# Windowed attention and a gated convolution in one kernel: its hand-written orders and the engines of its small copies are exchanged

## The chip, the cores and the metric

The kernel runs on one core of a Trainium2 chip. A core has five engines that run their own instruction streams and wait for each other by semaphores: TensorE (PE in the profile: matmuls and transposes by matmul, PEld its weight loads), VectorE (DVE), ScalarE (ACT), GpSimd (POOL) and SyncE (SP), which here issues every DMA. The metric is the device time of one execution in microseconds (us). The kernel before takes 554.26 us, the median of three runs (554.05, 554.26, 555.79).

## The reference

```
scores = (q @ k^T) / sqrt(64)                       # 8 batches, 8 heads, 576 tokens, 64 wide, fp32
scores = where(0 <= rel < 128, scores - slope[h] * |rel|, -1e9)   # rel = query - key position
attn   = exp(scores - max) / (sum + 1e-9)
x      = (attn @ v), heads joined                    # (8, 576, 512)
h      = max(x @ w_in, 0)                            # 512 -> 1024
conv   = sum_k conv_w[k] * h shifted by k - 1        # three taps along the tokens, zeros at a batch's ends
out    = (h * sigmoid(conv)) @ w_out                 # 1024 -> 512
```

## The kernel before

The 8 x 576 tokens are 36 tiles of 128 tokens for the attention and 18 chunks of 256 tokens for the second part. A chunk is worked in four steps, each on two blocks of 128 of the 1024 columns, so there are 72 steps; the text writes a step's number behind its piece.

**The attention of a tile.** q and k come by DMA (from tile 8 on in groups of nine blocks of 32 tokens, `rp_late`, 32 DMAs to a group, two buffers). DVE turns them over (`STREAM_TRANSPOSE`, L365, piece TQ), PE makes the scores of a tile in four PSUM tiles `sc` (L413, piece S), DVE masks each (L457 and L463, piece MP) and adds the bias with the maximum's work (L473, two instructions to a tile, piece MB), ACT takes the exponentials (L481, two instructions to a piece X), and a product with the reciprocal sums, on POOL from L501, normalizes (piece N). The weights are then turned over by a way through memory: DVE transposes them (L534, TE), a DMA writes them twice, 1 MB, into `scr` (L544, WE), eight DMAs to a pair of tiles read them back along a diagonal (L558, SE), POOL cuts them to the window (L568 and L572, CE), and PE multiplies with v (L591, AV). The first eight tiles take a shorter way with transposes on PE.

**The second part of a step.** PE makes the up-product `p` (L697, 12 matmuls to a block, 24 to a step, piece UH; L692 for the first four steps), as a sum of a high and two low parts of fp32, and ACT the relu `hh` (L709, HH). ACT takes the middle tap (L717, Z), DVE the two outer taps (L732, CA and CB, four instructions to a step), ACT the tanh that gives the sigmoid (L739, TH), DVE the gate (L747, GT), ACT the high part `gh` (L186, GH), POOL the low part `gl` (L768, GL), and PE the down-product `o` (L804, D). After four steps the chunk's result is copied to `ob` and stored (L830, OB). `zp`, which holds the taps, is one buffer: the next step's middle tap waits for the gate of this one. Scores, up-products and the attention's products all take turns in one pool of five PSUM tiles, so that a matmul into the next tile also waits for whoever reads the tile that is five turns older.

**What sets the order.** Nothing is scheduled by a planner: every engine runs its instructions as the program emits them. Three strings of pieces say what is emitted in which order, and one helper runs them:

```
emit(OPENING)
for t in range(FIRST, NT, 2):                 # FIRST = 8, NT = 36: 14 times, two tiles and four steps each
    emit(PERIOD, t, 2 * (t - FIRST) + 10, "P:")
emit(TAIL, NT, 2 * (NT - FIRST) + 10, "T:")
```

A number behind a name counts from t or from the step: in the period for t = 20, TQ4 is tile 24, WE3 tile 23 and UH4.1 the second block of step 38. The opening holds the first eight tiles, the splitting of the weights into high and low parts (pieces CL, RS, LW, V, H, W, from the weight DMAs F) and the first steps; LG4 issues the next four DMAs of a group. For a small copy or a cast that more than one engine can do, `pick(usual, other)` takes the second engine where the piece's name stands in the set `OTHER`.

Of the kernel before, what the change touches and what calls it, by code (L numbers as in the profile page):

```python
# [16 lines left out]
P = 128  # L17
# [5 lines left out]
def tile_alibi_window_attention_conv_glu(  # L23
# [265 lines left out]
    TURN = FIRST  # L289
# [86 lines left out]
    def window(t):  # L376
        return (t * P) % S, 1, 0
# [45 lines left out]
    def place(t, u, a):  # L423
# [11 lines left out]
        if t >= TURN:  # L435
            place_window(t, ps)
            return
# [30 lines left out]
    def add_bias(t, u, a):  # L468
        e, st, pss = sms[t, u]
        of = pss[a][:, :, BK:WIN] if t >= TURN else pss[a][:, :, window(t)[1], :]  # L470
# [383 lines left out]
    def emit(pieces, t=0, s=0, part=""):  # L854
# [16 lines left out]
        GH6 GH7 GH8 GL5 H14 H15 H16 H2 H5 H9 HH0.0 HH3.1 HH4 HH5 KC7 LW0 LW1 LW10 LW14 LW4 LW8 N2.0 N3.1 N8.0  # L871
        QV2.0 QV3.0 RL1.0 RL3.1 RL5.1 RL6.1 T:GH-1 T:GH0 T:GH1 T:GH2 T:GH3 T:GH4 T:GH5.0 T:GH5.1 T:GL-1 T:GL0
        T:GL4 T:GL5.0 T:HH0 T:HH2 T:HH4 T:HH5.1 T:XL-1 W11 W13 W14 W9 XH0 XH2 XH6
# [47 lines left out]
    AV-1 HH0 Z0.0 UH1.1 XA-1 UH1.0 XS-1 D-2 Z0.1 CA0.1 CA0.0 CB0.1 CB0.0 TH0 GT0 XH-1 XL-1 GH-1 XF-1 GL-1 HH1 Z1.1  # L921
    Z1.0 CA1.1 CA1.0 GH0 CB1.0 GL0 CB1.1 UH3.0 TH1 GT1 UH2.0 UH2.1 HH2 Z2.0 Z2.1 CA2.1 CA2.0 CB2.1 CB2.0 TH2 GT2 GH2
# [39 lines left out]
```

## Time and profile before

| | |
|---|---|
| median of three runs | 554.26 us |
| the profiled execution's own time | 554.5 us |
| its span, from the first instruction to the last | 552.8 us |
| PE busy | 546.0 us, 99% of the span |
| DVE, ACT, POOL busy | 446.8, 384.4, 342.5 us |
| share of the chain of waits on PE | 91% |
| granted clock of PE, mean | 0.999 |

The 1.7 us between the span and the execution's own time lie before the first and behind the last instruction. PE stands still for 6.8 us of the span, the time ahead of its first matmul and that of the last store among them.

### The profile page before, as it was taken

How to read it: one execution, taken by the hardware profiler on the slowest of the kernel's cores; microseconds unless marked ns; L12 is line 12 of the kernel's file. 1: busy time of each engine (PE TensorE's matmuls, PEld its weight loads, DVE VectorE, ACT ScalarE, POOL GpSimd, SP SyncE). 2: the span in 40 equal slices, each digit the busy share in tenths (PEclk: the TensorE clock that was granted, in tenths of full speed). 3: DMA queues.
4: the chain of work that ended last, by engine and by line, in shares of the span. 5: the costliest groups of instructions: out<-in, count | busy, mean ns of one | idle time of the engine just before them, and what ended most of it. 6: DMA issues, size and time to landing. Idle time of an engine off the chain costs nothing.

```text
span 552.8 us, 17956 instructions
## 1 busy us (share of the span) xinstructions
PE 546.0 (99%) x6689; PEld 479.2 (87%) x6689; DVE 446.8 (81%) x1505; ACT 384.4 (70%) x1149; POOL 342.5 (62%) x450
## 2 busy tenths in 40 slices
PE   9999999999999999999999999999999999999997
PEld 8788886988888888888888888898989898989986
DVE  8899999888789977887596987788879987665763
ACT  5899876775867676868586776767676777664441
POOL 1787977594656575666558493948473948483241
PEclk9999999999999999999999999999999999999999
DMA  9987764546776767767676768676768664540102
GB/s 209 229 242 204 202 104 81 164 156 169 157 205 142 231 156 205 184 205 169 183 201 175 196 178 207 163 219 184 190 176 205 179 162 148 159 155 1 39 0 78
DMA packets 206779, 91.39 MB, mean 165 GB/s; under 512 B 178380, under 2 KB 192996, under 8 KB 206692
## 3 DMA queue, kind: packets, MB, share of 16 engines
q1 hardware_dynamic: 206692, 90.24, 62.5%
q8 instruction: 53, 0.87, 0.7%
q14 instruction: 34, 0.28, 0.2%
HBM read 51.40 MB, written 38.80 MB: 163 GB/s over the span
## 4 chain that ended last, share of the span: by engine, by line
PE 91%; DMA 2%; DVE 2%; SPq 2%; issue 1%; ACT 0%; DVEq 0%
PE o L804 34%; PE p L697 33%; PE av L591 7%; PE sc L413 6%; PE p L692 3%; PE o L794 3%; PE av L631 3%; PE sc L398 2%; SPq L341 1%; DMA wst<-in_moe_w_in_dram 1%; PE pa L507 1%; PE pt L351 1%; DVE zp L732 1%; DMA rp_late<-in_q_dram 1%; SPq L315 0%
## 5 line engine op out<-in xcount | busy, mean ns | idle before, releaser
L697 PE MATMUL p<-ring,wi 128*128 128x256 f32 x1088 | 195.8, 282 | 0.7 <-ACT hh L709 0.7
L732 DVE SCALAR_TENSOR_TENSOR zp<-hh,cw,zp 128x256 f32<-128x256 f32 (+7 forms) x384 | 160.4, 418 | 29.2 <-ACT zp L717 19.6
L697 PEld LDWEIGHTS p<-ring,wi 128*128 128x128 f32 x1088 | 168.4, 188 | 4.9 <-ACT hh L709 1.1
L697 PE MATMUL p<-ring,wl 128*128 128x256 f32 x544 | 152.3, 280 | 0.0
L768 POOL TENSOR_TENSOR gl<-z,gh 128x512 fp32r<-128x512 f32 x63 | 81.5, 1294 | 100.9 <-ACT gh L186 68.4
L481 ACT ACTIVATE e<-e,st 128x128 f32<-128x128 f32 x288 | 111.8, 391 | 4.2 <-DVE st L473 3.1
L804 PE MATMUL o<-wo,gh 128*128 128x512 f32 x270 | 110.0, 407 | 0.0
L501 POOL TENSOR_TENSOR e<-e,st 128x512 f32<-128x512 f32 x69 | 72.2, 1056 | 58.9 <-DVE st L493 54.1
L804 PE MATMUL o<-wo,gl 128*128 128x512 f32 x270 | 105.7, 392 | 0.0
L804 PE MATMUL o<-wl,gh 128*128 128x512 f32 x270 | 105.2, 390 | 0.0
L697 PEld LDWEIGHTS p<-ring,wl 128*128 128x128 f32 x544 | 102.7, 189 | 0.0
L739 ACT ACTIVATE zp<-zp 128x512 f32<-128x512 f32 (+1 forms) x73 | 42.2, 578 | 62.9 <-DVE zp L732 61.5
L717 ACT ACTIVATE zp<-hh,cw 128x256 f32<-128x256 f32 x144 | 68.5, 476 | 20.0 <-DVE z L747 10.0
L473 DVE CUSTOM_DVE_ANT_0 e<-sc,bias 128x128 f32<-128x128 f32 x288 | 66.8, 284 | 1.7 <-PE pa L507 0.2
L747 DVE SCALAR_TENSOR_TENSOR z<-zp,hh 128x512 f32<-128x512 f32 (+1 forms) x73 | 49.0, 671 | 21.1 <-ACT zp L739 20.2
L804 PEld LDWEIGHTS o<-wo,gh 128*128 128x128 f32 x270 | 50.6, 188 | 16.6 <-issue 6.7
L804 PEld LDWEIGHTS o<-wo,gl 128*128 128x128 f32 x270 | 50.5, 187 | 11.5
L804 PEld LDWEIGHTS o<-wl,gh 128*128 128x128 f32 x270 | 50.8, 188 | 9.3
L709 ACT ACTIVATE hh<-p 128x512 f32<-128x512 f32 (+2 forms) x69 | 39.5, 572 | 25.2 <-PE p L697 20.3
L481 ACT ACTIVATION_READ_ACCUMULATOR e<-e,st 128x1 f32 x288 | 54.5, 189 | 0.0
L186 ACT CAST gh<-z 128x512 fp32r<-128x512 f32 x58 | 35.6, 614 | 15.3 <-DVE z L747 15.3
L572 POOL TENSOR_SCALAR_AFFINE_SELECT rr<-rr 128x512 f32<-128x512 f32 x56 | 40.2, 722 | 3.4
(131 smaller groups left out, 882.5 us busy)
## 6 DMA issues: line engine op xcount, KB each, us to landing
scr<-eb SPq DMA_DIRECT2D x28, 1024.0 KB, 5.1
rr<-scr SPq DMA_DIRECT2D x112, 128.0 KB, 3.7
out_dram<-ob SPq DMA_DIRECT2D x17, 512.0 KB, 3.4
rv<-in_v_dram SPq DMA_DIRECT2D x32, 256.0 KB, 3.4
rp_late<-in_k_dram SPq DMA_DIRECT2D x192, 36.0 KB, 2.9
rp_late<-in_q_dram SPq DMA_DIRECT2D x192, 36.0 KB, 2.2
wst<-in_moe_w_in_dram SPq DMA_DIRECT2D x8, 512.0 KB, 7.0
wst<-in_moe_w_out_dram SPq DMA_DIRECT2D x8, 512.0 KB, 4.8
```

The lines of the kernel that those rows point to most:

```text
L473: nc.vector.tensor_tensor_reduce(out=e[:, j, :], in0=of[:, g, :], in1=bias[:, u * HU + j, :], scale=-0.125, scalar=FAR, op0=ALU.add, op1=A ...
L481: nc.scalar.activation(out=e[:, j, :], in_=e[:, j, :], func=AF.Exp, bias=st[:, 0, j : j + 1], scale=-1.0, accum_out=st[:, 1, j : j + 1],)
L501: eng.tensor_tensor(out=e, in0=e, in1=st[:, 2, :].unsqueeze(2).to_broadcast([P, HU, P]), op=ALU.mult)
L572: nc.gpsimd.affine_select(out=r, in_=r, pattern=[[BK, 2], [0, H], [1, BK]], compare_op=ALU.is_ge, fill=0.0, base=q0, channel_multiplier=-1,)
L697: nc.tensor.matmul(ps, a[:, part], ring[:, i, cc, cols], start=cc == 0 and n == 0, stop=cc == NCC - 1 and n == 2)
L709: nc.scalar.activation(out=to, in_=ps, func=AF.Relu, scale=0.5)
L717: nc.scalar.activation(out=zps[s][:, ff, :], in_=hhs[s][:, ff, 1 : 1 + CW], func=AF.Copy, scale=cw[:, 1, f : f + 1])
L732: nc.vector.scalar_tensor_tensor(out=z[:, ff, a:cut], in0=hh[:, ff, a + kk : cut + kk], scalar=cw[:, kk, f : f + 1], in1=z[:, ff, a:cut], ...
L739: nc.scalar.activation(out=zps[s][:, ff], in_=zps[s][:, ff], func=AF.Tanh)
L747: nc.vector.scalar_tensor_tensor(out=zgs[s][:, ff], in0=zps[s][:, ff], scalar=1.0, in1=hhs[s][:, ff, 1 : 1 + CW], op0=ALU.add, op1=ALU.mult,)
L768: eng.tensor_tensor(out=gl, in0=zgs.pop(s), in1=as32(gh), op=ALU.subtract)
L804: nc.tensor.matmul(to, a[:, ff, ms], w[:, part], start=first and n == 0, stop=end and n == 2)
```

## The change

The three strings are replaced, and 23 names leave the set `OTHER` while 27 others come in. The constants `TURN`, `SOLO` and `FIRST` are all 8, so the edits to `scores`, `place` and `add_bias` decide as before. PE has 4638 instructions in both and SP 655 DMAs in both; on DVE, ACT and POOL the counts change by the copies that move (DVE 1507 to 1514, ACT 863 to 859, POOL 455 to 452). In the program after the change, the lines that the rows name are one higher up to the scores (L315 is L316, L365 is L366).

```
-    TURN = FIRST
+    TURN = 8
+    SOLO = 8
...
-        if t >= TURN:
-            if u == 0:
-                for half in range(2):
-                    scores_window(t, half)
+        if t >= FIRST:
+            for half in range(2) if t >= SOLO else (u,):
+                scores_window(t, half)
...
     OTHER = set(
-        GH6 GH7 GH8 GL5 H14 H15 H16 H2 H5 H9 HH0.0 HH3.1 HH4 HH5 KC7 LW0 LW1 LW10 LW14 LW4 LW8 N2.0 N3.1 N8.0
+        GH7 GH8 GL5 H1 H10 H11 H13 H14 H15 H3 HH0.0 HH3.1 HH4 HH6 HH9 LW1 LW4 LW8 LW9 N2.0 N4.0 N8.1 N9.1 QV2.0
...
     OPENING = """
-    LH0.0 LH0.1 LD1 F0 QU0.0 QU0.1 QV0.0 S0.0 MP0.0.0 F4 MP0.0.1 MB0.0.0 QV0.1 S0.1 LD2 MP0.1.1 LD3 MB0.0.1 MP0.1.0
+    LH0.0 F4 LH0.1 QU0.0 QV0.0 QU0.1 S0.0 LD1 MP0.0.0 MP0.0.1 MB0.0.0 MB0.0.1 QV0.1 S0.1 LD2 QU1.0 QV1.0 QU1.1 QV1.1
...
     PERIOD = """
-    OB0 HH0 Z0.0 MB2.0.1 MB2.0.0 X2.0.0 UH1.1 UH1.0 HH1 X2.0.1 CA0.0 AV-1 TQ3 CB0.0 XA-1 XS-1 AV0 LG4 GH-1 GL-1 N2.0
+    MB2.0.0 HH0 Z0.0 X2.0.0 GH-1 GL-1 UH1.0 UH1.1 MB2.0.1 X2.0.1 CA0.0 TQ3 CB0.0 HH1 LG4 LG4 N2.0 AV-1 XA-1 XS-1 AV0
...
     TAIL = """
-    AV-1 HH0 Z0.0 UH1.1 XA-1 UH1.0 XS-1 D-2 Z0.1 CA0.1 CA0.0 CB0.1 CB0.0 TH0 GT0 XH-1 XL-1 GH-1 XF-1 GL-1 HH1 Z1.1
+    UH1.0 AV-1 UH1.1 HH0 XA-1 XS-1 D-2 XH-1 Z0.0 XL-1 XF-1 UH2.0 GH-1 Z0.1 UH3.0 CA0.1 GL-1 CA0.0 UH2.1 CB0.1 CB0.0
```

In the period, PE's order changes only in that the two blocks of the first up-product change places. What moves on the other engines is shown at the end of the period for t = 18 and in the one for t = 20. On SyncE, before, at the end of the period (`rp11` is a group's tile, `scr21` the memory to which tile 21's weights are written):

```order
L315 DMA rp11_late_4600<-in_q_dram 32x9x32 x8
L830 DMA out_0_dram<-ob7_4839 128x2x512
L315 DMA rp11_late_4600<-in_q_dram 32x9x32 x4
L544 DMA scr21_4867<-eb21_4843 256x1x1024
L315 DMA rp11_late_4600<-in_q_dram 32x9x32 x4
L341 DMA rv23_5081<-in_v_dram 128x8x64
L315 DMA rp12_late_5103<-in_k_dram 32x9x32 x4
```

and after:

```order
L316 DMA rp11_late_4581<-in_q_dram 32x9x32 x8
L830 DMA out_0_dram<-ob7_4845 128x2x512
L316 DMA rp11_late_4581<-in_q_dram 32x9x32 x8
L544 DMA scr21_4881<-eb21_4860 256x1x1024
L342 DMA rv23_5079<-in_v_dram 128x8x64
L316 DMA rp12_late_5085<-in_k_dram 32x9x32 x4
L544 DMA scr22_5129<-eb22_5024 256x1x1024
```

The 1 MB write stood ahead of the last four q DMAs of the group; now it stands behind them, and with that nearer to the next 1 MB write. On VectorE, before, behind the transposes of tile 24 and the four outer taps of step 35 (`sc23_1_0` is one of the four score tiles of tile 23, `z35` the gate of step 35):

```order
L457 COPY_PREDICATED sc23_0_1_5036<-w_diag_117,sc23_0_1_5036 128x2x32
L463 COPY_PREDICATED sc23_0_1_5036<-w_after_139,neg_90 128x2x128
L457 COPY_PREDICATED sc23_1_0_5053<-w_diag_117,sc23_1_0_5053 128x2x32
L463 COPY_PREDICATED sc23_1_0_5053<-w_after_139,neg_90 128x2x128
L747 SCALAR_TENSOR_TENSOR z35_5145<-zp35_5077,hh3_166 128x512
L457 COPY_PREDICATED sc23_0_0_5035<-w_diag_117,sc23_0_0_5035 128x2x32
L463 COPY_PREDICATED sc23_0_0_5035<-w_after_139,neg_90 128x2x128
L473 ISA e23_0_5124,st23_0_5125<-sc23_0_1_5036,bias_142 128x128
L473 ISA st23_0_5125 128x1
L473 ISA e23_0_5124,st23_0_5125<-sc23_0_1_5036,bias_142 128x128
L473 ISA st23_0_5125 128x1
L473 ISA e23_0_5124,st23_0_5125<-sc23_0_0_5035,bias_142 128x128
```

and after, behind the same transposes and taps:

```order
L457 COPY_PREDICATED sc23_1_0_5048<-w_diag_117,sc23_1_0_5048 128x2x32
L463 COPY_PREDICATED sc23_1_0_5048<-w_after_139,neg_90 128x2x128
L473 ISA e23_1_5066,st23_1_5067<-sc23_1_0_5048,bias_142 128x128
L473 ISA st23_1_5067 128x1
L473 ISA e23_1_5066,st23_1_5067<-sc23_1_0_5048,bias_142 128x128
L473 ISA st23_1_5067 128x1
L747 SCALAR_TENSOR_TENSOR z35_5160<-zp35_5081,hh3_166 128x512
L473 ISA e23_0_5071,st23_0_5072<-sc23_0_1_5031,bias_142 128x128
L473 ISA st23_0_5072 128x1
L473 ISA e23_0_5071,st23_0_5072<-sc23_0_1_5031,bias_142 128x128
L473 ISA st23_0_5072 128x1
L457 COPY_PREDICATED sc23_0_0_5030<-w_diag_117,sc23_0_0_5030 128x2x32
```

The masks of `sc23_0_1` (L457, L463) are gone from here: they stand ahead of the transposes of tile 24 now. The bias of `sc23_1_0` moved ahead of the gate, and the mask and bias of `sc23_0_0` came to the end. On ScalarE, before, in the same stretch (`e23` are the weights of tile 23, `hh0` and `hh1` the relus of steps 36 and 37):

```order
L481 ACTIVATE e23_1_5071,st23_1_5072<-e23_1_5071,st23_1_5072 128x128 x2
L739 ACTIVATE zp35_5077<-zp35_5077 128x512
L709 ACTIVATE hh0_163<-p36_5108 128x2x256
L717 ACTIVATE zp36_5141<-hh0_163,cw_153 128x256
L186 CAST gh35_5147<-z35_5145 128x512
L717 ACTIVATE zp36_5141<-hh0_163,cw_153 128x256
L709 ACTIVATE hh1_164<-p37_5154 128x2x256
L481 ACTIVATE e23_0_5124,st23_0_5125<-e23_0_5124,st23_0_5125 128x128 x2
L481 ACTIVATE e23_1_5071,st23_1_5072<-e23_1_5071,st23_1_5072 128x128 x2
L492 ACTIVATE st23_1_5072<-st23_1_5072 128x4
L739 ACTIVATE zp36_5141<-zp36_5141 128x512
```

and after:

```order
L717 ACTIVATE zp36_5157<-hh0_163,cw_153 128x256 x2
L186 CAST gh35_5162<-z35_5160 128x512
L709 ACTIVATE hh1_164<-p37_5144 128x2x256
L481 ACTIVATE e23_0_5071,st23_0_5072<-e23_0_5071,st23_0_5072 128x128 x2
L481 ACTIVATE e23_1_5066,st23_1_5067<-e23_1_5066,st23_1_5067 128x128 x4
L492 ACTIVATE st23_1_5067<-st23_1_5067 128x4
L739 ACTIVATE zp36_5157<-zp36_5157 128x512
L481 ACTIVATE e23_0_5071,st23_0_5072<-e23_0_5071,st23_0_5072 128x128 x2
L492 ACTIVATE st23_0_5072<-st23_0_5072 128x4
```

The exponentials of `e23_1` stand together behind the relu of step 37 now, where two of the four stood ahead of the tanh of step 35 before; and the two middle taps of step 36 stand together ahead of the cast of `gh35`.

## Rows read from the trace of the kernel before

**Rows 1.** Busy time of the engines, share of the span, instructions (the profile's page, part 1)

```profile
PE 546.0 (99%) x6689; PEld 479.2 (87%) x6689; DVE 446.8 (81%) x1505; ACT 384.4 (70%) x1149; POOL 342.5 (62%) x450
```

**Rows 2.** Waits of PE: total us, times, longest us

```profile
PE pt L351 <- DVE st L473: 1.1, 1, 1.1
PE p L697 <- ACT hh L709: 0.7, 2, 0.4
```

**Rows 3.** Chain of waits: start us, us, what; once to a period

```profile
216.81 7.08 PE p L697 x60
...
245.08 7.08 PE p L697 x60
...
331.35 7.08 PE p L697 x60
```

**Rows 4.** Chain of waits ahead of the first stall

```profile
271.03 3.96 DMA rp_late<-in_q_dram
...
275.07 0.71 DVE qkT_all L365
```

**Rows 5.** Timeline of PE: start us, us, what [idle before, releaser]

```profile
278.29 0.28 PE L697 MATMUL p<-ring,wl 128*128 128x256 f32 x1
278.91 0.51 PE L697 MATMUL p<-ring,wi 128*128 128x256 f32 x2 [0.34 <-ACT hh L709]
...
307.85 0.51 PE L697 MATMUL p<-ring,wi 128*128 128x256 f32 x2 [0.36 <-ACT hh L709]
...
309.78 1.65 PE L413 MATMUL sc<-qkT_all 64*32 64x160 f32 x64 [0.24 <-DVE st L473]
```

**Rows 6.** Timeline of SP's queue, 267 to 309 us

```profile
268.33 3.23 SPq L315 DMA_DIRECT2D rp_late<-in_q_dram  x4
...
297.24 0.53 SPq L544 DMA_DIRECT2D scr<-eb  x1
297.80 3.91 SPq L315 DMA_DIRECT2D rp_late<-in_q_dram  x4
...
304.80 0.53 SPq L544 DMA_DIRECT2D scr<-eb  x1
```

**Rows 7.** DMA issues by kind: KB each, us to landing (page, part 6)

```profile
scr<-eb SPq DMA_DIRECT2D x28, 1024.0 KB, 5.1
...
rp_late<-in_q_dram SPq DMA_DIRECT2D x192, 36.0 KB, 2.2
```

**Rows 8.** Timeline of DVE around the second stall

```profile
304.28 0.45 DVE L365 STREAM_TRANSPOSE qkT_all<-rp_late 128x256 f32<-128x256 f32 x1 [3.11 <-DMA rv<-in_v_dram]
...
306.84 0.49 DVE L463 COPY_PREDICATED_SCALAR sc<-w_after,neg 128x256 f32 x1
...
309.14 0.28 DVE L473 CUSTOM_DVE_ANT_0 e<-sc,bias 128x128 f32<-128x128 f32 x1
```

**Rows 9.** Timeline of ACT in the same stretch

```profile
310.00 0.58 ACT L709 ACTIVATE hh<-p 128x512 f32<-128x512 f32 x1
310.48 0.39 ACT L481 ACTIVATE e<-e,st 128x128 f32<-128x128 f32 x1
```

**Rows 10.** The opening, timeline of DVE

```profile
14.10 0.67 DVE L188 COPY qkT_all<-pt 128x512 f32<-128x512 f32 x1
...
17.36 0.43 DVE L221 TENSOR_SCALAR wst<-wst 128x512 uint32<-128x512 uint32 x1 [1.29 <-DMA wst<-in_moe_w_in_dram]
```

**Rows 11.** The opening, chain of waits: from the up-products of step 1 on

```profile
36.23 3.68 PE p L692 x16
```

**Rows 12.** Windows: length; PE, PEld, DVE, ACT, POOL busy; PE clock; DMA share; GB/s

```profile
10.00:20.00 10.00, 8.83 (x98) 7.93 (x98) 8.64 (x53) 9.20 (x39) 4.65 (x6) 1.00 1.02 223
```

**Rows 13.** POOL's last selection ahead of tile 20's product, timeline

```profile
291.30 0.72 POOL L572 TENSOR_SCALAR_AFFINE_SELECT rr<-rr 128x512 f32<-128x512 f32 x1
```

**Rows 14.** Chain of waits, products of tiles 19 and 20

```profile
291.84 2.84 PE av L591 x128
```

**Rows 15.** Chain of waits, the end

```profile
548.14 1.42 PE o_last L804 x12
```

More of the change, by code (lines that the diff above doesn't have):

```diff
@@ L469, in add_bias @@
         e, st, pss = sms[t, u]
-        of = pss[a][:, :, BK:WIN] if t >= TURN else pss[a][:, :, window(t)[1], :]
+        of = pss[a][:, :, BK:WIN] if t >= FIRST else pss[a][:, :, window(t)[1], :]
         for g in range(NG):
@@ new lines, in tile_alibi_window_attention_conv_glu @@
+    I2 I2 CL4 F0 MP0.1.0 X0.0.0 MB0.1.0 X0.1.0 MP0.1.1 MB0.1.1 S1.0 S1.1 X0.0.1 MP1.1.0 MB1.1.0 I2 QU2.1 QU2.0
+    MP1.0.0 QV2.1 LW4 I1 X0.1.1 NR0 CL0 LW0 N0.1 N0.0 MP1.0.1 S2.1 T0.1 X1.1.0 MP1.1.1 I1 MB1.0.1 MB1.1.1 LD3 QU3.0
+    MB1.0.0 F1 QV2.0 X1.0.1 LW1 F2 T0.0 RL0.1 LD4 S2.0 MP2.0.1 X1.1.1 X1.0.0 NR1 SEL0.1 LV0 N1.1 QU3.1 RL0.0 I1 I1
+    N1.0 CL1 RS4 QV3.1 I2 MP2.1.0 T1.1 MB2.1.0 V4 P4 RS0 QV3.0 MP2.1.1 MB2.0.1 MP2.0.0 MB2.1.1 S3.1 RL1.1 SEL1.1
+    MP3.1.1 MP3.1.0 T1.0 MB2.0.0 RL1.0 MB3.1.1 W4 X2.1.1 F3 SEL0.0 MB3.1.0 CL2 S3.0 MP3.0.1 X2.1.0 X2.0.1 X2.0.0 V0
@@ new lines, in tile_alibi_window_attention_conv_glu @@
+    QV6.1 RS5 V5 MP5.0.1 MB5.0.1 RL3.0 QU6.0 UH3.0 HH0.1 Z0.0 W0 H7 Z0.1 HH3.0 X5.1.1 LV4 QV6.0 SEL3.0 F9 CA0.0 N4.1
+    F10 UH2.0 HH2.0 SEL3.1 CL9 CA0.1 CB0.0 CL10 LG4 RL4.0 SEL4.0 CB0.1 TH0 LD7 T4.1 RL4.1 S6.0 MP5.0.0 MB5.0.0 H2
+    X5.0.1 F12 LW9 MP6.0.1 MB6.0.1 X5.0.0 LG4 SEL4.1 MP6.0.0 S6.1 MB6.0.0 MP6.1.1 AV3 F11 W2 GT0 MB6.1.1 LG4 Z1.1
+    XH3 XL3 X5.1.0 AV4 Z1.0 RS10 CA1.0 LG4 XH4 CA1.1 GL0 CB1.1 H3 NR5 RS9 QU7.1 XL4 W3 MP6.1.0 LG4 LV5 N5.1 CB1.0
+    X6.0.0 LW10 MB6.1.0 CL11 V9 UH2.1 HH2.1 TH1 XF4 UH3.1 HH3.1 F13 LW11 H8 GT1 QV7.1 QU7.0 QV7.0 LG4 LG4 V10 H10 W8
@@ new lines, in tile_alibi_window_attention_conv_glu @@
+    Z2.0 F16 Z2.1 T5.1 F14 RL5.1 X6.1.1 CA2.0 UH4.1 UH4.0 HH4 LV6 H6 X6.1.0 CA2.1 LG4 CB2.0 CB2.1 S7.1 MP7.1.1 S7.0
+    MP7.0.1 TH2 MP7.0.0 GT2 CL12 CL15 UH5.1 UH5.0 W6 LG4 LG4 N5.0 MP7.1.0 W7 H5 D0 RS11 KC7 T5.0 Z3.1 SEL5.1 GL1
+    CL13 W5 UH6.0 RS12 CA3.1 CB3.1 V11 CL16 X6.0.1 N6.0 MB7.0.1 Z3.0 UH6.1 CA3.0 CB3.0 MB7.0.0 TH3 N6.1 LV8 LW12 GT3
+    GL3 V12 HH5 MB7.1.1 X7.0.0 TQ8 LG4 LG4 Z4.1 LW16 UH7.0 MB7.1.0 BW1 X7.0.1 CA4.1 Z4.0 CB4.1 H9 CL14 RL5.0 SEL5.0
+    X7.1.0 RS16 CA4.0 CB4.0 TH4 LW15 W10 UH7.1 LG4 LG4 LG4 T6.1 T6.0 LG4 LG4 LG4 V16 GT4 GL2 RL6.1 SEL6.1 LW14 D1
@@ new lines, in tile_alibi_window_attention_conv_glu @@
+    HH6 HH7 RL6.0 Z5.0 SEL6.0 Z5.1 RS13 CA5.0 CB5.0 N7.0 CA5.1 CB5.1 TH5 AV5 XH5 XL5 RS14 LW13 V14 LG4 LG4 LG4 V13
+    RS15 AV6 GT5 Z6.0 Z6.1 V15 H11 H16 S8.0 GH5 MP8.1.1 H14 X7.1.1 D2 D3 XH6 LG4 MB8.1.1 W16 T7.0 BW0 W9 MP8.1.0
+    MB8.1.0 TQ9 GH4 CA6.0 X8.1.0 XL6 UH8.0 CA6.1 CB6.0 MP8.0.0 CB6.1 UH8.1 MB8.0.0 LV9 W11 TH6 GT6 UH9.1 RL7.0
+    MP8.0.1 S9.0 Z7.1 CA7.1 CB7.1 H15 MB8.0.1 X8.1.1 N8.1 Z7.0 GL4 HH8 H12 GH6 W14 CA7.0 CB7.0 TE8.1 UH9.0 TH7 OB3
+    MP9.1.1 MB9.1.1 X9.1.1 H13 W13 MP9.0.1 W15 GL5 HH9 MP9.1.0 N7.1 MB9.0.1 UH10.0 X8.0.0 X8.0.1 N8.0 MP9.0.0
@@ L926, in tile_alibi_window_attention_conv_glu @@
+    CA2.1 CB2.1 CB2.0 TH2 GT2 GH2 GL2 HH3 Z3.1 CA3.1 Z3.0 CA3.0 CB3.0 CB3.1 TH3 GL1 HH5.1 GT3 GH3 GL3 UH4.0 HH4 Z4.0
+    CA4.0 CB4.0 D0 D1 OB1 Z4.1 CA4.1 UH5.0 D2 HH5.0 CB4.1 TH4 GT4 Z5.0 GH4 GL4 CA5.0 CB5.0 TH5.0 D3 D4 GT5.0 GH5.0
+    Z5.1 CA5.1 CB5.1 TH5.1 GT5.1 GH5.1 GL5.0 GL5.1 D5 OB5
     """
@@ L930, in tile_alibi_window_attention_conv_glu @@
         emit(OPENING)
-        for t in range(FIRST, NT, 2):
-            emit(PERIOD, t, 2 * (t - FIRST) + 10, "P:")
-        emit(TAIL, NT, 2 * (NT - FIRST) + 10, "T:")
+        for t in range(SOLO, NT, 2):
+            emit(PERIOD, t, 2 * (t - SOLO) + 10, "P:")
+        emit(TAIL, NT, 2 * (NT - SOLO) + 10, "T:")
 _INS = ["q", "k", "v", "moe_w_in", "moe_conv_w", "moe_w_out"]
```

61 lines of the change are left out of this document (19 added, 42 removed).

## Prediction

> **What bounds the kernel now.** The page's busy times come first: PE works 546.0 of 552.8 us, while DVE has 106 us to spare and ACT and POOL more [rows 1]. PE's work is the same after the change, so only its 6.8 us of standstill can shrink, and only new standstill can make the kernel slower. Of the 6.8 us, 3.2 lie behind the last matmul (548.14 + 1.42 = 549.56 against 552.8 [rows 15]). Next come PE's waits, which say where the rest is: one of 1.1 us on DVE in a transpose of the opening, and two, together 0.7 us, on the relu `hh` [rows 2]. The chain of waits says what such a stall costs, because one of its rows returns once to a period: 28.27 us lie between the first two of those shown (245.08 - 216.81), and the three periods behind them take 331.35 - 245.08 = 86.27 us instead of 3 x 28.27 = 84.81 [rows 3]. So 1.46 us are lost in the middle of the kernel, and no other period loses anything.
>
> Following the chain back from the first of these two stalls, one sees what ended last: the DMA of the last q blocks of a group, which landed 3.96 us after its issue, and behind it the transposes of tile 22, the outer taps, the tanh, the relu, and PE [rows 4]. PE's matmul at 278.91 follows one at 278.29 where matmuls of this shape otherwise start about 0.12 us apart, so this stall is 0.50 us [rows 5]. The second one begins at 307.85 in the same manner, goes on in the scores of tile 24 at 309.78 [rows 5], and is the rest, 1.46 - 0.50 = 0.96 us. Here DVE had stood idle for 3.11 us ahead of the transposes of tile 24, whose last four q DMAs were issued from 297.80 on, behind a 1 MB write issued at 297.24 [rows 6, 8]. (The wait names a DMA of v as the releaser; it landed at about the same time, and the transposes read only q and k.)
>
> **The change part by part.** The edits to the constants and branches change nothing, since all three constants are 8.
>
> *The write behind the loads.* The four q DMAs no longer stand behind the write. The least that this gives them is its issue time and the step to the next issue, 297.80 - 297.24 = 0.56 us [rows 6]. The most is that time and what the last load took too long: 3.96 against a median of 2.2 us to landing is 1.76 us [rows 4, 7], so 2.32 us in all. I call the gain x, between 0.56 and 2.32 us.
>
> The Trainium skill, "DMA: Bandwidth & Descriptors", in its section on queues, rings and completion order, says that each DMA engine takes the descriptors of a queue in ring order, by which the loads had to wait until the write's descriptors were worked off; the landing of 3.96 against 2.2 us agrees. The same page, in its section on why small descriptors are slow, speaks for the other end: runs below 512 bytes, as in these loads, pay for themselves wherever they stand. By the first rule both stalls go and the middle gives back 1.46 us; by the second x stays at 0.56 and it gives back 1.06.
>
> The first stall needs x > 0.50 us, and even the lower bound has that: -0.50 us. For the second, the order behind the transposes matters too. One mask pair (0.49 us for L463 and some 0.15 for L457) leaves the place behind them for DVE's idle time ahead of them [rows 8], which brings the gate of step 35 forward by 0.64 us; two bias instructions of 0.28 us each, now ahead of the gate, take up to 0.56 of that back. What ends last then is on ACT: the second half of the scores at 309.78 needs the PSUM tile that the relu of step 37 reads. That relu ran at 310.00 for 0.58 us [rows 9], and it still stands behind both middle taps of step 36 and the cast of `gh35`. So this stall shrinks by about x and no more than its 0.96 us: a gain between 0.56 and 0.96. I take 0.70, nearer the lower end, since the write's issue is certain and its drag on the landing only likely. The middle gives -0.50 - 0.70 = -1.20 us. If nothing changed in when the loads land, it would give 0; so the bounds are 0 and -1.46.
>
> *What the write pays.* It goes out up to 3.91 us later [rows 6], that is 3.65 us ahead of the next write instead of 7.56. A write lands after 5.1 us [rows 7], so it is there about 306.3; its data are read back only after the second write, which goes out at 304.80. The second write may be pushed by up to 5.1 - 3.65 = 1.45 us. I cost this at nothing; its cover is the time between the reading back and the selection on POOL, which is not shown to be tight, and the 1.24 us below.
>
> *The exponentials.* Two of them, 0.39 us each [rows 9], move to just ahead of the sums of `e23_1`, and one mask instruction goes ahead of DVE's second reciprocal. So the normalization of both halves, and the selections behind it on POOL, can end some 0.78 + 0.2 = 1.0 us later. Waiting for them is the product with v: POOL's last selection for tile 20 ended at 291.30 + 0.72 = 292.02, and PE took tile 20's half of the two products from 291.84 + 1.42 = 293.26 [rows 13, 14], a cover of 1.24 us. It holds by 0.2. That is in a period just behind a stall, where ACT is late anyway; elsewhere the cover should be no smaller. Cost: nothing, and if the cover goes, each tenth is paid in 14 periods.
>
> *The opening.* Here DVE is busy 8.64 of 10 us [rows 12], and what it does late PE gets late. PE's long wait ends a chain in which DVE stood 1.29 us for a weight block that landed then, at 17.36 [rows 10]. In the new order, the PSUM tiles that this transpose of PE needs are freed ahead of that weight's work, so the wait can go: -1.1 us at best [rows 2]. Against it stands DVE's load ahead of the first up-products: it takes on two copies of 0.67 us and gives up one of those and one of 0.43 [rows 10], +0.24 us if DVE is what sets the time. Laying out the new order piece by piece with the durations of before, I come to 35.9 us for the first of these products, and it is 36.07 now, just ahead of the chain's row at 36.23 [rows 11]. I take that, -0.2 us, between the bounds -1.1 and +0.24.
>
> *The end.* PE has no wait there now [rows 2], and the moved copies have their old cover: 0.
>
> *The sum.* -1.20 - 0.2 + 0 = -1.4 us. The profiled execution took 554.5 us itself, so 553.1 by its own time; it was 0.24 above the median of the runs. Against that median, 554.26 - 1.4 = **552.9 us**.
>
> **The rivals.** *A larger gain:* both stalls go entirely and the opening's wait too, 554.26 - 1.46 - 1.1 = 551.7 us. For it speaks that DVE's idle time ahead of the transposes was 3.11 us [rows 8], so that the loads have room to come earlier by the whole 2.32; against it, that another engine takes over in an opening in which ACT is busy 9.20 of 10 us [rows 12].
>
> *No change:* the loads come no earlier, because SP's queue is what is late. The last four took 3.91 us to issue, where those of the first stall took 3.23 [rows 6]; if the issue waits for room that all DMAs share, taking one write away from ahead of them only moves the waiting. Then the middle gives 0, the opening -0.2 to +0.24: 554.1 to 554.5 us. Against it: no other period has such a stall, though it has the same loads [rows 3].
>
> *Slower:* the exponentials. If the selections end more than 1.24 us later [rows 13, 14], the product with v waits in every one of the 14 periods. The two exponentials and the mask make 1.0; one more instruction ahead of them on ACT, as the cast of 0.6 us that now comes before, makes it 1.6, 0.3 to 0.4 beyond the cover. That is 14 x 0.3 = +4.2 us: 552.9 + 4.2 = 557.1 us. For it: POOL's selections are eight in a row without a gap, so a late start is not made up. Against: in the stretch around 310 us ACT had just waited itself, and where it isn't late the moved exponentials only fill its idle time (70% busy [rows 1]).
>
> **How the numbers follow.** The forecast's own case, a gain of 0.3 to 2.3 us (552.0 to 554.0), gets 50%; the larger gain (551.0 to 552.0) 14%; no change 19%; slower 17%, with its price anywhere from 1.7 us up. A measurement here tells 0.3%, 1.66 us, from no change: below 552.60 is faster, above 555.92 slower. Of the forecast's case about half, 24%, lies below 552.60, and with the larger gain that makes 38% faster; the other 26% with the 19% make 45% within; 17% slower. The range reaches from 551.1, which takes in most of the larger gain, to 556.2, which leaves out the greater part of the slower case; the likeliest case's own is 552.0 to 554.0.
>
> **What would show it.** In the chain of waits the row that returns should come every 28.27 us all the way, with 84.8 us for the three periods from 245 us on, and PE's waits on `hh` should be gone; the last q DMAs should be issued ahead of the write, and DVE's idle time ahead of the transposes should fall from 3.1 us to below 2.5. In the opening the wait of 1.1 us should be shorter or elsewhere, and the first up-product at 35.9. A wait of PE on POOL at L591 in many periods would prove the slower rival; a shorter DVE idle time without a shorter period would mean that the stall hung on something else; and a period that stays at 86.27 for three, with the loads landing as late as now, would prove that of no change.

## The result and the profile after

The changed kernel takes 558.31 us, the median of five runs (557.41 to 559.12); the kernel before took 554.26 beside it. The ratio is 1.0068 with a 95% interval of 1.0047 to 1.0089: it is slower, where 552.9 us and a small gain were forecast. The profiled execution took 557.41 us, 2.9 more than that of before, and its span is longer by as much, 555.7 against 552.8. It is the fastest of its five, so what is read from the traces below accounts for 2.9 of the 4.05 us between the medians.

The page after has almost the same work on PE [rows 1]; on DVE 7.5 us more for seven more instructions:

```profile
PE 546.5 (98%) x6689; PEld 479.5 (86%) x6689; DVE 454.3 (82%) x1512; ACT 381.0 (69%) x1145; POOL 339.5 (61%) x447
```

Where PE lost the time is best read from marks that both traces have. The chain of waits of before reaches the up-products of step 12, early in the first period, so (start us, us, what):

```profile
132.27 0.79 PE p L697 x5
```

and the one after so:

```profile
135.13 7.08 PE p L697 x60
...
219.47 7.08 PE p L697 x60
...
247.75 7.08 PE p L697 x60
```

Up to this mark the changed kernel is 2.86 us behind, 2.74 by the matmuls' own starts (132.22 and 134.96); the text counts this as the opening. At the later marks the lag is the same: 219.47 and 247.75 against 216.81 and 245.08 [rows 3], 2.7 us. From the first up-product of step 12 to the last matmul, before took 417.33 us and after 417.50. So the sum of period and end is unchanged, but two large terms cancel in it.

The one is the gain of the forecast. PE's waits on the relu [rows 2] are gone from the list of its waits, which now begins so (total us, times, longest):

```profile
PE av L591 <- DVE xx L605: 1.4, 1, 1.4
PE idle L72 <- DVE x_first L275: 1.1, 1, 1.1
PE p L697 <- DVE st L473: 0.6, 2, 0.4
PE pa L507 <- DVE e L501: 0.5, 1, 0.5
PE o L794 <- DVE wg L225: 0.4, 1, 0.4
```

DVE's timeline around the transposes of tiles 22 and 24, which answers to [rows 8], shows why: no idle time is left ahead of tile 22's, where DVE waited 3.61 us before, and 0.64 instead of 3.11 ahead of tile 24's last ones. Before:

```profile
275.07 0.71 DVE L365 STREAM_TRANSPOSE qkT_all<-rp_late 128x512 f32<-128x512 f32 x1 [3.61 <-DMA rp_late<-in_q_dram]
```

and after:

```profile
273.42 1.30 DVE L366 STREAM_TRANSPOSE qkT_all<-rp_late 128x512 f32<-128x512 f32 x2
...
304.35 0.45 DVE L366 STREAM_TRANSPOSE qkT_all<-rp_late 128x256 f32<-128x256 f32 x1 [0.64 <-DMA rp_late<-in_q_dram]
```

From step 12 to the tail PE's order differs by two blocks alone, so the starts of the same matmuls can be compared one by one. The lag of the changed kernel is 2.67 us ahead of the first old stall, 2.03 behind it and 0.77 behind the second: 1.89 us are won back.

The other term is a new wait, once, at the products with v of tiles 23 and 24. The chain of waits there:

```profile
337.71 0.76 SPq L316
338.52 5.70 DMA scr<-eb
344.23 3.22 DMA rr<-scr
...
347.67 0.73 POOL ll L568
...
350.69 1.64 PE av L591 x64
```

The 128 matmuls that took 2.84 us in one go before, as in [rows 14], stretch from 350.69 to 355.18, in two halves. Both wait for POOL's eight selections, which follow each other without a gap: the first half starts 0.05 us after the fourth has ended, the second 0.05 us after the eighth, at 352.84 + 0.72 = 353.56. The eighth ended at 348.74 + 0.72 = 349.46 before, so it is 4.10 us late. Timelines of POOL before, and of POOL and PE after:

```profile
348.74 0.72 POOL L572 TENSOR_SCALAR_AFFINE_SELECT rr<-rr 128x512 f32<-128x512 f32 x1
```

```profile
352.84 0.72 POOL L572 TENSOR_SCALAR_AFFINE_SELECT rr<-rr 128x512 f32<-128x512 f32 x1
```

```profile
353.61 0.32 PE L591 MATMUL av<-rr,rv 64*64 64x128 f32 x1 [1.35 <-DVE xx L605]
```

The profile names DVE's sum of the first half (L605) as the releaser of the second, but that ended at 353.62, no earlier than the second half began. In e1, e4, e7, e9 and e11 below, the second half starts 0.05 us after the eighth selection as well, in e1 and e4 0.6 to 0.9 us ahead of the end of that sum; in e12 alone it starts 0.55 us after it, and why is open. By the starts of the same matmuls the wait costs 1.93 us (the lag goes from 0.77 to 2.70), and 0.21 more are lost at the products of tiles 25 and 26. So the terms behind the mark are -0.08 us up to 140 us, -1.89, +1.93 and +0.21, in sum the 0.17 between 417.33 and 417.50.

The wait begins on SP's queue. Before, the two 1 MB writes and the reads stood so (timeline):

```profile
327.26 0.57 SPq L544 DMA_DIRECT2D scr<-eb  x1
327.87 3.24 SPq L315 DMA_DIRECT2D rp_late<-in_q_dram  x4
331.21 0.40 SPq L341 DMA_DIRECT2D rv<-in_v_dram  x1
331.71 2.02 SPq L315 DMA_DIRECT2D rp_late<-in_k_dram  x4
333.77 0.56 SPq L544 DMA_DIRECT2D scr<-eb  x1
334.38 3.22 SPq L315 DMA_DIRECT2D rp_late<-in_k_dram  x4
337.70 4.76 SPq L558 DMA_DIRECT2D rr<-scr  x8
```

and after:

```profile
328.97 4.46 SPq L316 DMA_DIRECT2D rp_late<-in_q_dram  x8
333.53 0.57 SPq L544 DMA_DIRECT2D scr<-eb  x1
334.19 0.56 SPq L342 DMA_DIRECT2D rv<-in_v_dram  x1
334.84 3.63 SPq L316 DMA_DIRECT2D rp_late<-in_k_dram  x4
338.52 0.56 SPq L544 DMA_DIRECT2D scr<-eb  x1
339.12 3.45 SPq L316 DMA_DIRECT2D rp_late<-in_k_dram  x4
342.67 3.76 SPq L558 DMA_DIRECT2D rr<-scr  x8
```

In both traces four loads right behind a 1 MB write take 3.2 to 4.1 us to issue, wherever the write stands; most groups of four with none just ahead of them take 1.8 to 2.9, here 2.02. Before, the q loads paid this. After, the k loads do, and behind them the second write and the reads wait in the same queue: the reads go out 4.97 us later, at 342.67, while PE is only 0.77 us later.

### The profile page after: what moved, and what is told of

Read it like the earlier page. It is cut to its first block, busy times and chain, and to the rows that moved or that the text cites. A ratio compares the mean times of both kernels' runs of the same rounds, so it can differ in the third digit from the quotient of the medians.

```text
span 555.7 us, 17950 instructions
## 1 busy us (share of the span) xinstructions
PE 546.5 (98%) x6689; PEld 479.5 (86%) x6689; DVE 454.3 (82%) x1512; ACT 381.0 (69%) x1145; POOL 339.5 (61%) x447
## 4 chain that ended last, share of the span: by engine, by line
PE 73%; DVE 10%; SPq 5%; POOL 4%; DMA 3%; ACT 2%; issue 2%; DVEq 0%; POOLq 0%; ACTq 0%
PE o L804 30%; PE p L697 27%; PE av L591 6%; PE sc L413 5%; SPq L316 5%; PE p L692 2%; DVE e L473 2%; DVE zp L732 2%; ACT e L481 1%; DMA rr<-scr 1%; DMA scr<-eb 1%; PE av L631 1%; PE sc L398 1%; DVE z L747 1%; POOL ll L568 1%
## 5 line engine op out<-in xcount | busy, mean ns | idle before, releaser
L501 POOL TENSOR_TENSOR e<-e,st 128x512 f32<-128x512 f32 x68 | 71.0, 1046 | 53.0 <-DVE st L493 52.5
L473 DVE CUSTOM_DVE_ANT_0 e<-sc,bias 128x128 f32<-128x128 f32 x288 | 69.7, 284 | 3.3 <-PE pa L507 1.7
L747 DVE SCALAR_TENSOR_TENSOR z<-zp,hh 128x512 f32<-128x512 f32 (+1 forms) x73 | 48.8, 669 | 11.9 <-ACT zp L739 10.8
L709 ACT ACTIVATE hh<-p 128x512 f32<-128x512 f32 (+1 forms) x68 | 38.8, 570 | 16.9 <-PE p L697 15.4
L591 PE MATMUL av<-rr,rv 64*64 64x128 f32 (+1 forms) x896 | 39.8, 246 | 1.6 <-DVE xx L605 1.4
```

The lines of the kernel that those rows point to most:

```text
L473: nc.vector.tensor_tensor_reduce(out=e[:, j, :], in0=of[:, g, :], in1=bias[:, u * HU + j, :], scale=-0.125, scalar=FAR, op0=ALU.add, op1=A ...
L501: eng.tensor_tensor(out=e, in0=e, in1=st[:, 2, :].unsqueeze(2).to_broadcast([P, HU, P]), op=ALU.mult)
L591: nc.tensor.matmul(pss[k][a * D : (a + 1) * D, h // 2, c : c + n], vraw[t - side][rows, h + a], sides_of[t][side][rows, c // BK : (c + n) ...
L747: nc.vector.scalar_tensor_tensor(out=zgs[s][:, ff], in0=zps[s][:, ff], scalar=1.0, in1=hhs[s][:, ff, 1 : 1 + CW], op0=ALU.add, op1=ALU.mult,)
```

## The experiments

All times are beside runs of the kernel before on the same chip. The two columns at the right are read from each profile: when PE begins the up-products of step 12 (132.22 us before), and how long it takes from there to its last matmul (417.33 before). They come from one execution each, and executions of one kernel lie up to 4.6 us apart (e11: 556.31 to 560.87). The same opening varied by 0.8 us (that of before: 131.46 to 132.22) and 1.0 us (the new one: 134.96 to 135.98) from one kernel's profile to another's, so a change of a few tenths is read at the wait itself. Of the times up to step 12 in e2 and e6, some 0.5 us are a wait at step 12 itself, for a ring copy on DVE, where the new opening meets the period of before.

| | us | ratio, 95% interval | step 12 begins | from there |
|---|---|---|---|---|
| changed kernel | 558.31 | 1.0068 (1.0047 to 1.0089) | 134.96 | 417.50 |
| e1, opening of before | 554.20 | 0.9997 (0.9985 to 1.0010) | 131.98 | 417.42 |
| e2, period of before | 557.63 | 1.0062 (1.0047 to 1.0076) | 135.98 | 417.12 |
| e3, write first | 557.83 | 1.0071 (1.0055 to 1.0087) | 135.11 | 417.61 |
| e4, before with write last | 554.46 | 1.0004 (0.9989 to 1.0018) | 131.46 | 416.40 |
| e5, first part new, write last | 554.70 | 1.0014 (0.9998 to 1.0030) | 132.87 | 415.43 |
| e6, second part new | 557.28 | 1.0062 (1.0044 to 1.0080) | 134.92 | 417.28 |
| e7, engines back | 559.63 | 1.0106 (1.0085 to 1.0128) | 136.06 | 418.64 |
| e8, weight later | 554.08 | 1.0006 (0.9994 to 1.0018) | 131.80 | 417.19 |
| e9, four moves | 558.82 | 1.0083 (1.0061 to 1.0106) | 135.69 | 417.19 |
| e10, half way | 554.61 | 1.0006 (0.9995 to 1.0016) | 131.50 | 417.59 |
| e11, DVE moves | 557.42 | 1.0059 (1.0035 to 1.0083) | 135.55 | 417.49 |
| e12, bias only | 557.52 | 1.0046 (1.0029 to 1.0063) | 134.12 | 418.61 |

**e1 and e2: which string costs.**

```
e1, against the changed kernel:
-    OPENING = new order; its names in OTHER
+    OPENING = order of before; its names in OTHER of before
e2, against the changed kernel:
-    PERIOD = new order
+    PERIOD = order of before
```

> The changed kernel with the opening of before (its order and the engines of its small copies), the period and the end as changed. Theory (the loss is in the opening): PE reaches the first period 2.7 to 2.9 us earlier, as in the kernel before, and the time is 558.3 - 2.7 = 555.6 us or less; with the two old stalls gone and the new one of 1.95 us still there, 554.0 to 555.6. Rival (the period is what costs): less than 1 us comes back, 557.3 us or more.

> The changed kernel with the period of before. Theory (the loss is in the opening): the opening keeps its 2.7 us, so 554.3 + 2.7 = 557.0 us, with the two waits on the relu back near 280 and 310 us and no wait of tile 23's and 24's products. Rival (the period costs): 555 us or less.

The opening it is: with that of before the whole loss is gone (554.20, beside 554.08 for the kernel before), with the period of before it stays (557.63 beside the same). e2 keeps a wait on the relu, one of 0.8 us instead of two, and has none on the selections, much as the theory had it.

**e3 and e4: the write alone.**

```
e3, end of the changed period:
-    ... LG4 CE2.1 LG4 LG4 CB3.1 LG4 TE3.1 TH3 UH4.0 GL2 TE3.0 N4.1 WE3 GT3
+    ... LG4 CE2.1 CB3.1 TE3.1 TH3 UH4.0 GL2 TE3.0 N4.1 WE3 LG4 LG4 LG4 GT3
e4, end of the period of before:
-    ... MP4.0.0 WE3 LG4 GH2 CE2.1 LG4 LG4 GT3 GL2 XF-1 N4.1
+    ... MP4.0.0 LG4 GH2 CE2.1 LG4 LG4 WE3 GT3 GL2 XF-1 N4.1
```

> The changed kernel with one edit in the period: the last 1 MB write of the weights stands ahead of the last four q DMAs again. Theory (the write's place makes both the old stalls and the new one): the wait of the products of tiles 23 and 24 on the selections goes (-1.9 us), the waits on the relu come back (+0.5 to +1.5): 557.0 to 558.0 us. Rival (the new orders of DVE and ACT make the selections late): the wait of those products stays, and with the old stalls on top 558.5 us or more.

> The kernel before with one edit in the period: the last 1 MB write of the weights goes behind the last q DMAs. Theory (the write's place): both waits on the relu go (-1.46 us) and a wait of a product with v on the selections appears later (up to +1.9): 552.8 to 554.7 us. Rival (the order of DVE is needed too): the second stall, at 308 us, stays at more than half its 0.96 us, and no wait on the selections appears: 553.5 us.

e4 fits the theory: both waits on the relu are gone, and the new one is there, on the selections.

```profile
PE av L591 <- POOL rr L572: 0.7, 1, 0.7
```

The balance is 0.93 us in the profile, which is that of the fastest of its twelve executions (552.81), and nothing that the times can tell. e3 fits by half. The wait on the selections is gone. But the waits on the relu did not come back, though DVE again stands idle ahead of both transposes, for 1.75 and 1.46 us. Either the new order of DVE lets the loads be late without hurting, which is the rival's point turned round, or PE, which is 2.3 us later there than in the changed kernel, comes late enough; that is open. In their place another wait of 0.6 us appears near 190 us, of PE on POOL's small cast into the ring (L665). It also stands in e1 and e12, with the write last, and the three periods with it are 1.0 to 1.7 us longer; its cause is open.

The write's place alone does not decide whether the wait on the selections comes. e5 below has the period of e4, and its profile has neither that wait nor those on the relu: there the reads go out 0.49 us earlier than in e4 (337.40 against 337.89) and PE comes to the products 1.4 us later. The write last makes the reads late; whether PE notices hangs on when PE arrives.

**e5, e6 and e8: where in the opening.**

```
e5, before:  OPENING = new order through S3.1, the rest in the old one; engines likewise
             PERIOD as in e4
e6, before:  OPENING = old order through S4.1, the rest in the new one; engines likewise
e8, before:
-    ... RS4 X1.1.1 F1 CL1 LW1 MP2.1.1 MP2.0.0 MP2.0.1 NR1 ... V4 QU3.1 MB2.1.1 I1 ...
+    ... RS4 X1.1.1 F1 CL1 MP2.1.1 MP2.0.0 MP2.0.1 NR1 ... V4 QU3.1 MB2.1.1 LW1 I1 ...
```

> The kernel before with two edits: its opening goes in the new order, with the new engines of the copies, up to the scores S3.1 (22 us) and in the old one behind that; and in the period the last 1 MB write stands behind the last q DMAs, as in the run before. Theory (the new opening gains 0.4 us up to there, where PE's wait of 1.1 us is gone, and loses behind it): PE is 0.3 to 0.9 us ahead of the kernel before at 130 us, and the time 553.0 to 553.8. Rival (work that was put off in the first 22 us is what costs later): PE is 0.5 us or more behind at 130 us, 554.5 or more.

> The kernel before with its opening in the old order up to the scores S4.1 (30 us), and in the new order with the new engines behind that; period and end of before. Theory (each wait of the new order costs by itself where it stands): the waits of the new order behind 31 us are there, 2.86 - 0.95 = 1.9 us, so 556.1 us. Rival (the new order's loss is a lag of DVE that comes from its first 30 us and is handed on): 554.8 or less.

> The kernel before with one edit in the opening: the first step on the second weight block (the DVE instruction that stood 1.29 us waiting for its DMA at 17.36 us) goes behind the bias instructions that free the PSUM tiles for QU3.0. Theory (the gap is given back later, as DVE sets the time behind it as well): QU3.0's wait of 1.18 us goes, but PE is less than 0.5 us ahead at 130 us: 553.8 to 554.3. Rival (the gap is a plain loss): 1.0 us ahead all the way, 553.1 us.

e6 reaches step 12 2.70 us later than the kernel before. Of that, 0.26 us were there at the first up-product (36.33 against 36.07), and 0.44 come in the wait at step 12 that the changed kernel does not have. The 2.0 left arise between the two, where the theory took 1.9 and the changed kernel loses 2.04, and with the same waits at the same pieces (QU6.1, UH6.0, D2, UH10.0). So 2.0 of the 2.74 us aren't handed on from the first 30 us: the new order and the new engines behind them make them. The other 0.70 us the changed kernel has lost by its first up-product, at 36.77. e5 is the rival's: half a microsecond ahead at 22 us, PE lost 1.0 us in the transpose QU4.0 right behind the seam, on DVE's copy for the early attention:

```profile
PE pt L351 <- DVE rl L188: 0.9, 1, 0.9
```

e8 shows that the wait of 1.1 us [rows 2] is no plain loss: without it PE is 1.0 us ahead at 18.6 us and 0.3 at 21.8, since it then waits in the scores for the same engine. The 0.42 us that are left at step 12 fit the theory but lie within what one opening varies by. The wait itself varies too: it is 0.5 us in e1 and e4, which have the opening of before.

**e7: the engines of the copies.**

```
against the changed kernel, five names leave OTHER:
-    QV2.1 QV4.1 W1 W5 W10
```

> The changed kernel with five small operations taken from DVE again: the copies QV2.1 and QV4.1 on ScalarE and the subtractions W1, W5 and W10 on GpSimd, as before. Theory (it is the engines: DVE got more than it can hide): PE's waits in T2.0 (0.5 us), at UH6.0 (0.65) go, 1.2 us come back: 557.1 us. Rival (it is the order on DVE, whoever does the copies): those waits stay at more than half, 557.8 us or more.

What the rival forecast came: both waits stay at more than half (0.70 us at T2.0, 0.59 at UH6.0), and it is slower still, 559.63. Its reason holds at most for the first, though. At UH6.0 PE no longer waits for the bias but for the low part of the weights that POOL subtracts later, and a new wait of 1.2 us on a normalization appears in the first 20 us:

```profile
PE pa L507 <- POOL e L501: 1.2, 1, 1.2
...
PE p L697 <- POOL wl L244: 0.4, 1, 0.4
```

Order and engines fit each other; the loss isn't the sum of the moved copies.

**e9: the pieces of PE.**

```
against the changed kernel, in OPENING:  QU6.1 behind UH0.1;  UH6.0 UH6.1 behind UH7.1;
                                         D4 ahead of UH10.0;  V13 ahead of V14
```

> The changed kernel with four local moves in the new opening, engines and all else as changed: on PE, the transpose QU6.1 goes behind the up-product UH0.1, the two blocks of UH6 behind those of UH7, and the down-product D4 ahead of the up-product UH10.0; on DVE, the weight step V13 goes ahead of V14. Theory (each wait is the place of one piece in an order, and costs by itself): the waits of PE at QU6.1 (0.43 us), UH6.0 (0.65), D2 (0.5) and UH10.0 (0.35) go and 1.5 to 1.9 us come back: 556.4 to 556.8 us. Rival (DVE's lag is what costs, and PE meets it at the next piece whichever that is): less than 0.8 us comes back, 557.5 or more.

The rival's, clearly. Two of the waits stay with the same length at whichever piece now stands there; that at D2 stays (0.36 us idle instead of 0.43), and at UH10.0's old place D4 now waits 0.34 us for a copy on ACT. After, PE's timeline has them at the transposes QU6.1 and at UH6.0:

```profile
43.60 0.66 PE L352 MATMUL pt<-ident_r,rp 128*128 128x128 f32 x4 [0.26 <-DVE st L473]
...
74.97 0.47 PE L697 MATMUL p<-ring,wi 128*128 128x256 f32 x2 [0.41 <-DVE st L473]
```

and in e9 at UH0.1 and at UH7.0:

```profile
43.78 0.92 PE L692 MATMUL p<-x_first,wg 128*128 128x258 f32 x3 [0.26 <-DVE st L473]
...
75.43 0.47 PE L697 MATMUL p<-ring,wi 128*128 128x256 f32 x2 [0.46 <-DVE st L473]
```

In these two places, whichever matmul comes next takes the next of the five PSUM tiles, and that is the one whose bias DVE has not done yet.

**e11 and e12: the place on DVE.**

```
e12, against the changed kernel, in OPENING:  MB7.0.1 MB7.0.0 right behind MP7.0.0
e11: the same, and LW13 V13 ahead of XH5
```

> The changed kernel with moves on DVE alone, in two places of the new opening: the bias instructions MB7.0.1 and MB7.0.0 go right behind their masks, ahead of the gate of step 2, W5, V11 and the taps of step 3 (they ran at 73.0 and 74.3 us, where the kernel before had them at 67.9 and 71.3); and the weight step V13 (with the ACT step LW13 that it needs) goes ahead of the ring copies XH5 and XL5. Theory (DVE's order sets the opening, so that what PE waits for must come early on DVE): the waits at T5.0 and UH6.0 (0.65 us) and at D2 (0.5) go, and PE is 0.9 to 1.2 us earlier at 130 us: about 557.2 us. Rival (DVE has too much to do, and the wait only moves to what was put behind): PE is less than 0.5 us earlier at 130 us, 557.8 or more.

> The first half of the run before alone: the changed kernel with the bias instructions MB7.0.1 and MB7.0.0 right behind their masks. Theory (DVE's order sets the opening): the wait of 0.65 us at T5.0 and UH6.0 goes, no new one takes its place, and PE is 0.5 to 0.9 us earlier than in the changed kernel at 100 us: 557.5 to 557.8 us. Rival (the wait moves to what was put behind): what is gained at UH6.0 is lost again by D5.

e12 fits the theory up to 100 us. After, DVE did a gate, a mask, a subtraction W5, taps and V11 ahead of the bias:

```profile
68.82 0.69 DVE L747 SCALAR_TENSOR_TENSOR z<-zp,hh 128x512 f32<-128x512 f32 x1
...
69.75 1.64 DVE L244 TENSOR_TENSOR wl<-wg,wi 128x512 fp32r<-128x512 f32 x1
71.31 1.00 DVE L732 SCALAR_TENSOR_TENSOR zp<-hh,cw,zp 128x256 f32<-128x256 f32 x2
72.22 0.78 DVE L225 SCALAR_TENSOR_TENSOR wg<-wg,wst 128x512 uint32<-128x512 uint32 x1
...
73.01 0.25 DVE L473 CUSTOM_DVE_ANT_0 e<-sc,bias 128x128 f32<-128x128 f32 x1
```

In e12 the bias begins at 68.98, and PE goes from the transposes into UH6.0 without a wait, at 74.48. PE's order is that of the changed kernel, so the starts can be compared: 0.68 us are won here, 0.26 at the products at 87 us and 0.11 at D2, after 0.2 lost ahead, and PE is 0.84 us earlier at step 12.

```profile
68.98 0.28 DVE L473 CUSTOM_DVE_ANT_0 e<-sc,bias 128x128 f32<-128x128 f32 x1
...
70.75 0.80 DVE L244 TENSOR_TENSOR wl<-wg,wi 128x512 fp32r<-128x512 f32 x1
```

```profile
74.48 0.48 PE L697 MATMUL p<-ring,wi 128*128 128x256 f32 x2
```

That no new wait takes its place holds for the opening alone: the wait near 190 us makes a period 1.55 us longer in this profile, and the profiled execution (557.67) is no faster than the changed kernel's. The ratios are 1.0046 and 1.0068, and their intervals overlap (1.0029 to 1.0063 and 1.0047 to 1.0089). So the gain is shown at the wait and not by the time. e11 shows the other side: with V13 moved too, the wait at D2 went, and one of 1.5 us came at the scores of tile 8, which wait for the ring copy that V13 had been put ahead of (the step needs LW13 from ACT, and DVE stands in order behind it).

```profile
PE sc L413 <- DVE ring L659: 1.5, 1, 1.5
```

**e10: a try for the best.**

```
against before:  LW1 as in e8;  in PERIOD  LG2 WE3 LG2  for  WE3 LG4
```

> The kernel before with two edits, as a try for the best: the weight step LW1 in the opening later, as in the earlier run; and the last 1 MB write of the period between the last four q DMAs, two ahead of it and two behind. Theory (a write half way gives the loads enough and takes too little from the reading back): neither the waits on the relu near 280 and 308 us nor a wait of a product on the selections, 1.4 us less in the middle and 0.3 in the opening: 552.3 to 552.9 us. Rival (each place of the write only chooses which of the two is late): one of them stays with more than 0.5 us, 553.3 or more.

The rival's: both waits on the relu are still there, 1.0 us in all. The two q loads left behind the write took 2.71 us to issue, where four without one ahead took 2.02. No version beat the kernel before.

```profile
297.43 0.52 SPq L544 DMA_DIRECT2D scr<-eb  x1
298.00 2.71 SPq L315 DMA_DIRECT2D rp_late<-in_q_dram  x2
```

## Why the prediction was wrong

**The write behind the loads: right, and its size too small.** Both old stalls went, 1.89 us against the 1.20 taken. The first was 0.64 us, not 0.50, as the matmuls right behind the gap start late as well; the second was 1.25, not 0.96. One of the three periods between the marks of [rows 3] is shorter than 28.27 us by itself (in e4, without stalls, PE took 27.83 from 244.13 to 271.96 us), so the difference from 3 x 28.27 hid 0.44 of them. e4 shows that the write's place removes the stalls. It does not follow that it alone does: in e3, with the write first, they are gone too.

**What the write pays: wrong.** It was costed at nothing, with a push of at most 1.45 us on the second write. The step missed that SP is one queue: the slow issue behind a write is not saved, it moves to the k loads and to all that is issued behind these. The write landed after 5.70 us, not far from 5.1 [rows 7], so the landing was not the term that was off; the second write went out 4.75 us later (338.52 against 333.77), the reads 4.97 and the eighth selection ended 4.10 later. The cover taken, 1.24 us, was not far off either: at tile 24 the selection had ended 1.50 us ahead of PE before. It could not hold 4.10 us less the 0.77 by which PE is later, and the wait of 1.93 us follows once, at tiles 23 and 24. e4 has such a wait with the write last, e3 none with the write first; e5 has the write last and PE later, and none. The rival "no change" had this reason, that taking the write away only moves the waiting, and looked for it at the wrong end.

**The opening: wrong, and it is the result.** -0.2 us was taken, with +0.24 as the worst; it is +2.74. The sum counted DVE's moved copies up to the first up-products and had no term behind them. In the trace after, PE enters these at 36.77 us, where 35.9 was laid out and 36.07 was before: the wait of 1.1 us went, as forecast, but others came, the longest at T2.0 for a product that DVE makes:

```profile
27.11 0.63 PE L507 MATMUL pa<-ident_r,e 128*128 128x128 f32 x4 [0.54 <-DVE e L501]
```

Behind the first up-products, where the sum had no term, PE waits four times more up to 110 us (QU6.1, UH6.0, D2, UH10.0) for a bias or a weight step on DVE; from start to start these cost 0.43, 0.65, 0.50 and 0.36 us, and with the 0.70 ahead they make 2.64 of the 2.74. e6 shows that these four waits arise behind 30 us, e9, at two of them, that they aren't a matter of PE's own order, e7 that they aren't the copies alone, and e12, at one of them, that it is where the bias stands on DVE. That the others have the same cause is only likely: for D2, e11 removed the wait and paid more elsewhere. The 0.70 us ahead are read from the trace and were not tested.

**DVE's prices.** The copies were priced at 0.67 us, but the subtraction W5, moved to DVE in the stretch behind, took 1.64 us beside POOL's work (see the end). It stood ahead of the bias that PE waited for.

**The exponentials (the slower rival): not seen.** No wait of PE on a product with v appears in every period, only the one at tiles 23 and 24, and that comes from the reads. Its remark that the selections follow without a gap, so that a late start is not made up, is what sets the length of that wait. That the time of the slower case, 557.1, was near is chance; its mechanism was not the one.

**The end: right.** The lag of 2.91 us at 500 us is the same at the last matmul.

## What to carry to other kernels

Where PE takes PSUM tiles in turn, a late reader of one tile stops whatever comes next; at the two waits where PE's order was changed that did not help, and at the one where the reader was moved on its own engine it did. A move in a DMA queue that is busy all the time makes late what now stands behind the slow transfer, so follow the queue to the next wait that it feeds, and ask how much slack that has. And sum over the whole stretch whose order changes, not to the first mark where it seems level.

## What was not expected of the hardware

The same DVE instruction can take longer beside GpSimd's. The subtraction at L244 took 0.68 to 0.69 us all four times in the kernel before, where POOL did nothing beside it. In the changed kernel DVE runs six of them. The two that began with POOL idle took 0.68 and 0.69; the four that began while a POOL instruction ran took 0.97 to 1.64, the longest being W5, and each ended 0.54 to 0.56 us after that instruction of POOL. In e12 W5 took 0.80, where it began 1.04 us behind POOL's subtraction. POOL's timeline of the changed kernel there:

```profile
68.56 1.04 POOL L501 TENSOR_TENSOR e<-e,st 128x512 f32<-128x512 f32 x1
69.55 1.29 POOL L244 TENSOR_TENSOR wl<-wg,wi 128x512 fp32r<-128x512 f32 x1
70.78 1.08 POOL L375 COPY qkT_all<-qkT_all 128x512 f32<-128x512 f32 x1
```

DVE's W5 ran from 69.75 to 71.39 and so ended 0.55 us after POOL's subtraction (70.84); in e12 it began a microsecond later and also ended 0.54 us after it. POOL's copy, which came next, took 1.08 us, where its mean before was 0.62. The gate on DVE at 68.82 (L747), which reads one of its two inputs from PSUM, took its usual 0.69 us beside POOL's product at 68.56. All 41 gates of full size that began beside a POOL instruction took 0.65 to 0.71.

The Trainium skill, "SBUF — State Buffer", in its section on the two separate sides, says that DVE with two inputs from SBUF and GpSimd share one pair of ports as a lock that one of them holds for a whole instruction. These traces agree: the subtraction, with two inputs in SBUF, ends by the end of POOL's instruction, not by its own start, POOL's next one gives way in turn, and the gate, with one input in SBUF, is not held up. What moves from GpSimd to DVE can so cost, beside its own time, what is left of the GpSimd instruction that it meets, here 1.09 us.
